# Attention and token/channel mixer on one core: batch 1's channel product by seven half-size products, and a new order at the close of that stage

## The chip, the cores and the metric

The kernel runs on one core of a Trainium2 chip. Of the core's engines, TensorE (PE) multiplies matrices into PSUM, VectorE (DVE) and ScalarE (ACT) read PSUM and write SBUF, GpSimd (POOL) issues the loads of the inputs here, and SyncE (SP) issues the transposing transfers and the stores. The metric is the device time of one launch in microseconds (us). Before the change the median of three runs was 354.32 us (354.26 to 354.45).

## The reference, cut to what matters

There are 8 batches of 12 heads, 448 tokens and 64 features per head; the model width is 768, the token layer is 256 wide and the channel layer 1536.

```python
scores = q @ k.T / sqrt(64) - log(448)
x = sigmoid(scores) @ v                        # per head, then heads side by side: 448 x 768
h = relu(x.T @ w_tok1) @ w_tok2                # mixes tokens, 448 -> 256 -> 448
u = x + h.T
out = u + relu(u @ w_ch1) @ w_ch2              # mixes channels, 768 -> 1536 -> 768
```

The kernel takes its inputs as float32, computes in float16 with float32 accumulation, and writes float32.

## The kernel before, in words

**Cycles.** A cycle is one third of a batch (four heads), so there are 24, numbered c, with batch b = c // 3 and third u = c % 3. The tiles are placed by hand, and every engine carries out its instructions in the order in which the code issues them; nothing is reordered by a planner. Cycle c computes the scores of (b, u) in seven groups (`qk`, L178: four matmuls into a PSUM tile of two banks, then a sigmoid on ACT), the product with v of the cycle before (`av`, L200, PSUM tiles xa, copied to xT by DVE), the token layer of two cycles before (`tok_tail` and `tok1`, tiles tk, ReLU on ACT), and its way back (`ytrans`, L302, tiles yt, which DVE adds to xT to give ut).

**Channel layer.** When the three thirds of a batch are in ut, its first channel product gives h2 = relu(u w_ch1), and its second product gives the output. The second product is spread over the next batch's cycles, one output pair per cycle (`ch2_pair`, L575), and the last 64 tokens go to `ch2_last` (L610).

**Two forms of the first product.** Batches 0 and 1 do it directly: `ch1` (L334) takes one of 12 blocks of 128 channels and makes six matmuls of 448 columns for it (batch 0 partly with 64 x 64 quarters). The later batches use `ch1_seven` (L432), a scheme of the Strassen kind: both matrices are cut in halves, the weights' sums s1, s2, s4 and one difference are made once (`weight_sums`, L398), the tokens' sums once per batch (`token_sums`, L418), and seven products of half the size replace eight. Each product n has three parts a, b, c of 256 channels, so 18 matmuls of 224 columns. Parts a and b share a two-bank tile of the scores' PSUM ring; c and the single parts take one of four other banks. The products 1, 6, 7, 4 are accumulated one on the other in one tile and 5, 3 in a second one, so each waits until the value before it has been copied out: 1, 6 and 5 by ACT into tiles pt, 7 and 3 by DVE with an addition and a ReLU, 4 by a ReLU on ACT. `ORDER` (L931) says in which order the parts run.

**PSUM.** The eight banks are two score tiles of two banks, and four single banks m0 to m3. `bank` (L84) hands these out: first by the written list `OPENING_BANKS`, then in rotation from `at_bank`, which the code sets at places. A new tile in a bank waits until the last reader of the tile before it is done.

**Cycles 6 to 8** (L935 to L987) run between the opening and the steady loop. `work` deals out the pieces of `pending` between the scores: in cycles 6 and 7 the rest of batch 0's second product (20 pieces), in cycle 8 the whole of batch 1's first product (24 half blocks). With each piece one entry of `copies` is carried out (the relayouts of k and q of batch 3 on DVE and their transposes on SP, `through_dma`, L143), or else one of `early`, the nine weight sums. The other three, `late`, change part of c1 in place, which batch 1's direct product still reads, and run in cycle 9.

**Steady loop** (L989 on). In each third cycle of a batch the output pair and the last tokens come first, then the sevens; `ytrans` stands between the sevens' 3c and 4c. The next cycle opens with two score groups and the first turn of an output pair in banks 2 and 3. `gated_loads` (L857) lets POOL start the loads for later batches after it has copied two columns of the freshly transposed q.

Of the kernel before, what the change touches and what calls it, by code (L numbers as in the profile page):

```python
# [13 lines left out]
SUB = mybir.AluOpType.subtract  # L14
# [9 lines left out]
NU = 3  # L24
NS = 224
BY_GROUP = [0, 1, 6, 7, 2, 3, 8, 9, 4, 5, 10, 11]
OPENING_BANKS = "20130130130130213021302130213021313021213021302130202130123102302132132032"


@with_exitstack  # L30
def kernel(
# [13 lines left out]
    B, H, S, E = q.shape  # L45
# [4 lines left out]
    NCB = CC // 128  # L50
# [17 lines left out]
    c1 = pc.tile([128, NDB, CC], FP16, name="c1")  # L68
# [13 lines left out]
    at_bank = [0]  # L82
# [95 lines left out]
    def qk(b, u, j):  # L178
        att[b, u, j] = pa.tile([128, 2, S], FP16, tag="att", bufs=10, name=f"att_{b}_{u}_{j}")
        ps = pp.tile([128, 2, 512], FP32, tag="qk", bufs=2, name=f"qk_{b}_{u}_{j}")  # L180
        for g in range(2):
            for hi in range(2):
                nc.tensor.matmul(  # L183
                    out=ps[64 * g : 64 * g + 64, hi, 0:S],
                    lhsT=tr[b, "k"][64 * hi : 64 * hi + 64, u, j, 64 * g : 64 * g + 64],
                    rhs=tr[b, "q"][64 * hi : 64 * hi + 64, u, :, 64 * g : 64 * g + 64],
                    start=True,
                    stop=True,
                )
        nc.scalar.activation(  # L190
            out=att[b, u, j][:, :, :],
            in_=ps[:, :, 0:S],
            func=SIGMOID,
            bias=bias_t[:, :],
            scale=att_scale,
        )
# [3 lines left out]
    def av(b, u, j0=0, j1=NJ):  # L200
        if j0 == 0:
            xa[b, u] = [
                bank([128, 512], FP32, f"xa_{b}_{u}_{g}")
                for g in range(2)
            ]
        ps = xa[b, u]
        for j in range(j0, j1):
            for g in range(2):
                for hi in range(2):
                    nc.tensor.matmul(  # L210
                        out=ps[g][64 * hi : 64 * hi + 64, 0:S],
                        lhsT=raw[b, "v"][64 * g : 64 * g + 64, u, hi, j, :],
                        rhs=att[b, u, j][64 * g : 64 * g + 64, hi, :],
                        start=(j == 0),
                        stop=(j == NJ - 1),
                    )
        if j1 == NJ:
            for g in range(2):
                nc.vector.tensor_copy(  # L219
                    out=xTs[b % 2][:, u, g, 0:S], in_=ps[g][:, 0:S]  # L220
                )
            if NU * b + u >= N_FIRST:
                nc.vector.tensor_copy(
                    out=xTs[b % 2][:, u, :, S:512], in_=xTs[b % 2][:, u, :, S - 64 : S]
                )
# [172 lines left out]
    def weight_sums():  # L398

        low, high = slice(0, NU), slice(NU, NDB)  # L400
        first, second = slice(0, MC), slice(MC, CC)
        s1, s2, s4 = sums

        def one(out, in0, in1, op):
            return [
                lambda d=d: nc.vector.tensor_tensor(
                    out=out[:, d, :], in0=in0[:, d, :], in1=in1[:, d, :], op=op
                )
                for d in range(NU)
            ]  # L410

        return [
            *one(s1, c1[:, high, second], c1[:, low, second], ADD),
            *one(s2, s1, c1[:, low, first], SUB),
            *one(s4, c1[:, high, first], s2, SUB),
        ], one(c1[:, low, second], c1[:, low, first], c1[:, low, second], SUB)

    def token_sums(b, u0=0, u1=NU):  # L418

# [316 lines left out]
    def pieces_ch1(b, cb0=0):  # L736
        for cb in range(cb0, NCB):
            for d in range(0, NDB, 3):
                yield 3 * S, lambda cb=cb, d=d: ch1(b, cb, d, d + 3)

    def pieces_ch2(b, groups):
        for t, half in groups:
            for n in range(0, NCB, 3):
                yield 3 * DH, lambda t=t, half=half, n=n: ch2(b, t, half, n, n + 3)

    def pieces_last(b):
        for n in range(0, NCB, 3):
            yield 3 * DH, lambda n=n: ch2_last(b, n, n + 3)
# [121 lines left out]
    ONE_RUN = 3 * NU  # L870
# [3 lines left out]
    for c, cb in ((N_FIRST, 3), (N_FIRST + 1, 8)):  # L874
# [3 lines left out]
        copies = []  # L878
# [49 lines left out]
            load(2, "v", v, 1, NU)  # L928
            gated_loads(b)

    ORDER = "1ab 2a 2b 1c 6ab 5ab 2c 6c 5c 7ab 3ab 7c 4ab 3c"  # L931
    SEVENS = [(int(x[0]), x[1:]) for x in ORDER.split()]
    pending, copies = [], []
    early, late = weight_sums()
    for c in range(2 * NU, ONE_RUN):  # L935
        b, u = divmod(c, NU)
        before, ahead = divmod(c - 1, NU), divmod(c - 2, NU)


        if c in (2 * NU, 2 * NU + 2):  # L940
            first = c
            if c == 2 * NU:
                pending, shares = [*pieces_ch2(0, by_half[2:]), *pieces_last(0)], [15, 15]
            else:
                pending, shares = list(pieces_ch1(1)), [30]
            total = sum(w for w, f in pending)
            spent = 0

        def work(share):
            goal = 3 * sum(shares[: c - first]) + share * shares[c - first]  # L950
            done = 0
            while pending and spent + done < total * goal / 90:
                w, f = pending.pop(0)
                f()
                done += w
                if copies:
                    copies.pop(0)()
                elif early:
                    early.pop(0)()
            return done  # L960

        qk(b, u, 0)
        qk(b, u, 1)
        av(*before)
        xtrans_dma(*before)
        qk(b, u, 2)
        if c == 2 * NU + 2:
            copies += through_dma(3, 0)[NU + 1 :]
        spent += work(1)
        qk(b, u, 3)  # L970
        qk(b, u, 4)
        tok_tail(*ahead)
        tok1(*ahead, with_scores=True)
        if c == 2 * NU + 1:
            copies = through_dma(3, 0)[: NU + 1]
        spent += work(2)
        if c == 2 * NU + 2:
            utrans(b - 1)
        qk(b, u, 5)
        qk(b, u, 6)  # L980
        spent += work(3)
        if c + 1 == ONE_RUN:
            at_bank[0] = 0
        ytrans(*ahead)
        if u == 2:
            gated_loads(b)
    assert not copies and not pending and not early  # L987

    for c in range(ONE_RUN, N_CYCLES):  # L989
        b, u = divmod(c, NU)  # L990
        before, ahead = divmod(c - 1, NU), divmod(c - 2, NU)

        X, Y = 2, 0
        at_bank[0] = X
        turn0, turn1, rest = ch2_pair(b - 2, u)
        part = len(turn1) * 2 // 3
        qk(b, u, 0)
        qk(b, u, 1)  # L1000
        for f in turn0:
            f()
        qk(b, u, 2)
        if copies:
            copies.pop(0)()
            copies.pop(0)()
        if u == 2:
            utrans(b - 1)
        at_bank[0] = Y
        av(*before, 0, 4)  # L1010
        qk(b, u, 3)
        av(*before, 4, NJ)
        xtrans_dma(*before)
        if u == 2:
            token_sums(b - 1)
        qk(b, u, 4)
        for f in turn1[:part]:
            f()
        qk(b, u, 5)
        for f in turn1[part:]:  # L1020
            f()
        at_bank[0] = Y
        tok_tail(*ahead)
        qk(b, u, 6)
        tok1(*ahead, with_scores=True)
        rest()
        while late:
            late.pop(0)()
        if u == 1 and copies:
            copies.pop(0)()  # L1030
            copies.pop(0)()
        if u == 0 and LATER < b + 1 < B or u == 1 and b + 1 == LATER:
            copies = through_dma(b + 1, 0)
        if u == 2:
            at_bank[0] = Y + 1
            for w, f in pieces_last(b - 2):
                f()
            step = ch1_seven(b - 1, (1, 3, 0, 2, 0))
            for at, (n, gs) in enumerate(SEVENS):
                step(n, gs)  # L1040
                if copies and at in (1, 3):
                    copies.pop(0)()
            ytrans(*ahead, (2, 0))
            step(4, "c")
        else:
            at_bank[0] = Y
            ytrans(*ahead)
        if u == 2 and b + 1 < B:
            gated_loads(b)
    assert not copies  # L1050
# [25 lines left out]
    token_sums(B - 1, 2, NU)  # L1076
    at = at_bank[0]
    m = [(at + n) % 4 for n in range(4)]
    step = ch1_seven(B - 1, (m[2], m[3], m[0], m[1], m[0]))
    for n, gs in SEVENS:  # L1080
        step(n, gs)
    at_bank[0] = m[1]
    ch2(B - 1, 0, 0, 0, 6)
    step(4, "c")
    at_bank[0] = m[2]
    ch2(B - 1, 0, 0, 6, NCB)
    for t, half in groups[1:]:
        for n in range(0, NCB, 3):
            ch2(B - 1, t, half, n, n + 3)
# [32 lines left out]
```

## Time and profile before

| | us |
|---|---|
| median of three runs | 354.32 |
| profiled execution, its own time | 354.0 |
| its span on the core | 352.2 |
| cycles 6 to 8, first score to the first of cycle 9 | 63.30 to 102.55 |
| one steady cycle, c = 16 | 191.39 to 199.69 |
| the seven products in cycle 11, without yt | 129.32 to 140.87 and 141.62 to 142.20 |
| last batch's tail, first seven to the end of PE's work | 321.31 to 348 |

A row of the timeline gives the start of a group of instructions, how long it lasted, the engine, the line of the code, the operation with the tiles that it writes and reads, and the count; in brackets stands how long the engine was idle before it, and what it waited for. A matmul's recorded duration is its passage through the array; how far apart matmuls are shows in the distance of starts. The granted clock of TensorE was 1.00 in all the stretches between 64 and 108 us.

### The profile page before, as it was taken

What the parts mean: (1) busy time and instruction counts of PE and PEld (TensorE: products, weight loads), DVE (VectorE), ACT (ScalarE), POOL (GpSimd) and SP (SyncE); (2) the same over time, 40 slices, a digit from 0 to 9 for tenths busy, and PEclk for the clock granted to TensorE, in tenths of its full rate; (3) what the DMA queues carried; (4) which work ended last, traced back from release to release, by engine and by line L of the source; (5) the groups of instructions that cost most, each with busy time, mean ns of one, the idle gap of its engine ahead of it and who ended that gap; (6) DMA issues with size and microseconds to landing.
All of it is one profiled execution on the core that took longest, in us unless ns stands there. A gap on an engine that the chain in (4) does not pass through costs nothing.

```text
span 352.2 us, 10131 instructions
## 1 busy us (share of the span) xinstructions
PE 342.4 (97%) x4423; PEld 237.2 (67%) x4423; DVE 199.7 (57%) x395; ACT 205.1 (58%) x263; POOL 56.9 (16%) x98
## 2 busy tenths in 40 slices
PE   7999999999999999999999999999999999999995
PEld 4655565555556679656886679766886679557953
DVE  3476558656546566458575566558563366518621
ACT  4996844566258854888348854888348853111400
POOL 8893430220040000400040000300010000000000
PEclk9999999999999999999999999999999999999999
DMA  7999999999999597998979597999984390055214
GB/s 118 171 179 200 206 204 199 166 208 251 169 173 193 90 171 162 159 170 154 201 113 195 133 183 160 164 163 158 206 106 94 85 157 24 5 117 110 50 45 112
DMA packets 104379, 52.16 MB, mean 148 GB/s; under 512 B 76432, under 2 KB 101264, under 8 KB 104336
## 3 DMA queue, kind: packets, MB, share of 16 engines
q1 hardware_dynamic: 78944, 29.70, 47.3%
q0 software_dynamic: 25168, 21.50, 40.1%
q8 instruction: 34, 0.56, 0.6%
q10 hardware_dynamic: 224, 0.33, 0.3%
q14 instruction: 9, 0.07, 0.1%
HBM read 43.45 MB, written 11.01 MB: 155 GB/s over the span
## 4 chain that ended last, share of the span: by engine, by line
PE 77%; DMA 7%; DVE 6%; POOL 4%; ACT 2%; issue 2%; DVEq 0%; ACTq 0%; POOLq 0%
PE c L364 11%; PE c L537 10%; PE c_ab L487 9%; PE qk L183 7%; PE xa L210 7%; PE c L341 7%; PE c L598 5%; PE c L622 5%; PE c_c L487 5%; PE tk L286 5%; DVE h L517 4%; PE yt L309 3%; DMA c<-in_moe_w_ch_dram 3%; DMA xn<-xT 2%; DMA w<-in_moe_w_tok_dram 2%
## 5 line engine op out<-in xcount | busy, mean ns | idle before, releaser
L190 ACT ACTIVATE att<-qk,att_bias 128x896 f16<-128x896 f32 x168 | 155.7, 1015 | 46.9 <-PE qk L183 46.4
L183 PE MATMUL qk<-tr_q,tr_k 64*64 64x448 f16 x672 | 58.9, 356 | 0.5 <-ACT att L190 0.2
L219 DVE CAST xT<-xa 128x448 f16<-128x448 f32 x48 | 27.7, 618 | 40.1 <-PE xa L210 40.1
L364 PE MATMUL c<-c,h 64*64 64x384 f16 x960 | 47.1, 323 | 1.1 <-DVE ut L316 1.0
L560 DVE TENSOR_TENSOR o<-un,c 128x384 f32<-128x384 f16 x42 | 23.3, 554 | 41.8 <-PE c L598 20.7
L487 PEld LDWEIGHTS <-c 128*128 128x128 f16 x432 | 41.0, 98 | 2.9 <-issue 1.8
L210 PE MATMUL xa<-att,raw_v 64*64 64x448 f16 x672 | 40.3, 349 | 0.2 <-DVE ut L316 0.2
L537 PE MATMUL c<-c,h 128*128 128x384 f16 x216 | 37.9, 326 | 0.6 <-DVE ut L316 0.5
L364 PEld LDWEIGHTS <-h 64*64 64x64 f16 x960 | 30.0, 107 | 12.3 <-issue 2.1
L183 PEld LDWEIGHTS <-tr_k 64*64 64x64 f16 x672 | 21.3, 105 | 18.8 <-issue 12.1
L508 ACT ACTIVATE pt_ab<-c_ab 128x896 f32<-128x896 f32 x18 | 16.5, 917 | 29.0 <-PE c_ab L487 29.0
L487 PEld LDWEIGHTS <-sum 128*128 128x128 f16 x324 | 31.1, 98 | 0.0
L537 PEld LDWEIGHTS <-h 128*128 128x128 f16 x216 | 20.3, 98 | 15.2 <-issue 2.1
L316 DVE TENSOR_TENSOR ut<-xT,yt 128x448 f16<-128x448 f16 x48 | 27.4, 613 | 2.4 <-PE yt L309 2.4
L210 PEld LDWEIGHTS <-raw_v 64*64 64x64 f16 x672 | 21.8, 107 | 10.3 <-issue 1.1
L859 POOL COPY gate<-tr_q 128x2 f16<-128x2 f16 x6 | 1.4, 239 | 168.9 <-DMA tr_q<-rel_q 168.9
L341 PE MATMUL c<-ut,c 128*128 128x448 f16 x120 | 24.6, 353 | 0.4 <-DMA c<-in_moe_w_ch_dram 0.4
L300 ACT ACTIVATE h<-tk 128x256 f16<-128x256 f32 x42 | 14.2, 408 | 16.6 <-PE tk L286 16.6
L598 PE MATMUL c<-c,h 128*128 128x384 f16 x120 | 22.0, 326 | 0.0
L309 PE MATMUL yt<-w,h 128*128 128x448 f16 x96 | 21.9, 353 | 0.0
L286 PE MATMUL tk<-xn,w 128*128 128x256 f16 (+1 forms) x156 | 21.8, 274 | 0.1
L352 DVE TENSOR_SCALAR h<-c 128x448 f16<-128x448 f32 x24 | 14.5, 621 | 10.9 <-PE c L341 10.1
(86 smaller groups left out, 402.5 us busy)
## 6 DMA issues: line engine op xcount, KB each, us to landing
out_dram<-o SPq DMA_DIRECT2D x48, 192.0 KB, 3.1
c<-in_moe_w_ch_dram POOLq DMA_DIRECT2D x4, 1152.0 KB, 15.8
raw_k<-in_k_dram POOLq DMA_DIRECT2D x10, 336.0 KB, 7.7
raw_q<-in_q_dram POOLq DMA_DIRECT2D x10, 336.0 KB, 11.2
raw_v<-in_v_dram POOLq DMA_DIRECT2D x10, 336.0 KB, 5.7
out_dram<-o SPq DMA_DIRECT2D x15, 96.0 KB, 2.4
raw_q<-in_q_dram POOLq DMA_DIRECT2D x12, 112.0 KB, 5.0
raw_k<-in_k_dram POOLq DMA_DIRECT2D x12, 112.0 KB, 5.1
```

The source lines that it names most:

```text
L183: nc.tensor.matmul(out=ps[64 * g : 64 * g + 64, hi, 0:S], lhsT=tr[b, "k"][64 * hi : 64 * hi + 64, u, j, 64 * g : 64 * g + 64], rhs=tr[b, " ...
L190: nc.scalar.activation(out=att[b, u, j][:, :, :], in_=ps[:, :, 0:S], func=SIGMOID, bias=bias_t[:, :], scale=att_scale,)
L210: nc.tensor.matmul(out=ps[g][64 * hi : 64 * hi + 64, 0:S], lhsT=raw[b, "v"][64 * g : 64 * g + 64, u, hi, j, :], rhs=att[b, u, j][64 * g : ...
L219: nc.vector.tensor_copy(out=xTs[b % 2][:, u, g, 0:S], in_=ps[g][:, 0:S])
L286: nc.tensor.matmul(out=ps[tcb], lhsT=w1[rows, t, cols], rhs=xn[b, u][rows, :, t, :], start=(t == 0 and not with_scores), stop=(t == (2 if ...
L309: nc.tensor.matmul(out=ps[:, 0:S], lhsT=h1[b, u][:, tcb, g, :], rhs=w2[:, tcb, :, :], start=(tcb == 0), stop=(tcb == 1),)
L316: nc.vector.tensor_tensor(out=uts[b % 2][:, db, 0:S], in0=xTs[b % 2][:, u, g, 0:S], in1=ps[:, 0:S], op=ADD)
L341: nc.tensor.matmul(out=ps[:, 0:S], lhsT=c1[:, BY_UNIT[d], 128 * cb : 128 * cb + 128], rhs=uts[b % 2][:, BY_UNIT[d], 0:S], start=(d == 0), ...
L364: nc.tensor.matmul(out=ps[p][m : m + 64, 0:n], lhsT=lhsT(p, part, m), rhs=rhs(p, part), start=(first and turn == 0), stop=(last and turn = ...
L487: nc.tensor.matmul(out=ps[:, g, p, :], lhsT=weights[n][:, d, 128 * cb : 128 * cb + 128], rhs=moving[n][:, d, :], start=(n in (1, 5, 2) and ...
L537: nc.tensor.matmul(out=ps[:, 0:DH], lhsT=h2[b][:, BY_GROUP[cb], 128 * t : 128 * t + 128], rhs=c2[:, BY_GROUP[cb], cols], start=(cb == 0), ...
L598: nc.tensor.matmul(out=ps[p][:, 0:DH], lhsT=h2[b][:, BY_GROUP[n], 128 * t : 128 * t + 128], rhs=c2[:, BY_GROUP[n], DH * p : DH * p + DH], ...
```

## The change

Batch 1's first channel product goes through `ch1_seven` as well, at the end of cycle 8. For that all twelve weight sums are made in cycles 6 to 8, one for each piece of work that has no relayout to carry out, and the token sums of batch 1 are made in cycle 8. Batch 0's twenty output pieces are dealt over the three cycles 6, 7 and 8 instead of two. The banks of these cycles are no longer taken from the written list: xa, tk and yt start at bank 0 each time, and the output groups alternate between banks 3 and 2.

In all stages of sevens 7c is moved ahead of 3ab, and 4c is the last of the sevens, ahead of `ytrans`. The single parts' banks change from (1, 3, 0, 2, 0) to (2, 3, 0, 1, 0) (c's two chains, then 2a, 2b, 2c), and yt takes banks 0 and 1 instead of 2 and 0. The output pair of the next cycle keeps banks 2 and 3; the tiles that it follows there are now c's two chains. In the tail 4c stands ahead of the first output group instead of in its middle.

```diff
-OPENING_BANKS = "20130130130130213021302130213021313021213021302130202130123102302132132032"
+OPENING_BANKS = "201301301301302130213021302130213130212130213021302021301"
...
             *one(s4, c1[:, high, first], s2, SUB),
-        ], one(c1[:, low, second], c1[:, low, first], c1[:, low, second], SUB)
+            *one(c1[:, low, second], c1[:, low, first], c1[:, low, second], SUB),
+        ]
...
-    ORDER = "1ab 2a 2b 1c 6ab 5ab 2c 6c 5c 7ab 3ab 7c 4ab 3c"
+    ORDER = "1ab 2a 2b 1c 6ab 5ab 2c 6c 5c 7ab 7c 3ab 4ab 3c 4c"
...
+    def sevens(b, banks=(2, 3, 0, 1, 0)):
+        step = ch1_seven(b, banks)
+        for at, (n, gs) in enumerate(SEVENS):
+            step(n, gs)
+            if copies and at in (1, 3):
+                copies.pop(0)()
...
-    early, late = weight_sums()
+    early = weight_sums()
+    lane = [0]
...
-        if c in (2 * NU, 2 * NU + 2):
+        if c == 2 * NU:
             first = c
-            if c == 2 * NU:
-                pending, shares = [*pieces_ch2(0, by_half[2:]), *pieces_last(0)], [15, 15]
-            else:
-                pending, shares = list(pieces_ch1(1)), [30]
+            pending, shares = [*pieces_ch2(0, by_half[2:]), *pieces_last(0)], [10, 10, 10]
...
                 w, f = pending.pop(0)
+                if len(pending) % 4 == 3:
+                    lane[0] ^= 1
+                at_bank[0] = 2 + lane[0]
                 f()
...
+        at_bank[0] = 0
         av(*before)
...
+        at_bank[0] = 0
         tok_tail(*ahead)
...
             utrans(b - 1)
+            token_sums(b - 1)
         qk(b, u, 5)
         qk(b, u, 6)
         spent += work(3)
-        if c + 1 == ONE_RUN:
-            at_bank[0] = 0
+        if u == 2:
+            sevens(b - 1)
+        at_bank[0] = 0
         ytrans(*ahead)
...
         rest()
-        while late:
-            late.pop(0)()
...
-            step = ch1_seven(b - 1, (1, 3, 0, 2, 0))
-            for at, (n, gs) in enumerate(SEVENS):
-                step(n, gs)
-                if copies and at in (1, 3):
-                    copies.pop(0)()
-            ytrans(*ahead, (2, 0))
-            step(4, "c")
-        else:
-            at_bank[0] = Y
-            ytrans(*ahead)
+            sevens(b - 1)
+        at_bank[0] = Y
+        ytrans(*ahead)
...
-    step = ch1_seven(B - 1, (m[2], m[3], m[0], m[1], m[0]))
-    for n, gs in SEVENS:
-        step(n, gs)
+    sevens(B - 1, (m[2], m[3], m[0], m[1], m[0]))
     at_bank[0] = m[1]
-    ch2(B - 1, 0, 0, 0, 6)
-    step(4, "c")
-    at_bank[0] = m[2]
-    ch2(B - 1, 0, 0, 6, NCB)
+    for n in range(0, NCB, 3):
+        ch2(B - 1, 0, 0, n, n + 3)
```

## The prediction

> **What bounds the kernel now.** I read the page's engine shares first, then TensorE's timeline around the change, then what DVE and the transfers do at the places where TensorE waits. PE below is TensorE.
>
> ```profile
> PE 342.4 (97%) x4423; PEld 237.2 (67%) x4423; DVE 199.7 (57%) x395; ACT 205.1 (58%) x263; POOL 56.9 (16%) x98
> PE 77%; DMA 7%; DVE 6%; POOL 4%; ACT 2%; issue 2%; DVEq 0%; ACTq 0%; POOLq 0%
> ```
>
> PE is the bound, so a column of matmul taken off it counts, and so does each PE gap. PE's timeline (start, us, line, output<-inputs, count): batch 1's first channel product in cycle 8, and the same product of batch 2 in sevenths, closed by yt and product 4c:
>
> ```profile
> 86.09 4.71 PE L341 MATMUL c<-ut,c 128*128 128x448 f16 x24
> 92.01 4.70 PE L341 MATMUL c<-ut,c 128*128 128x448 f16 x24
> 97.15 4.71 PE L341 MATMUL c<-ut,c 128*128 128x448 f16 x24
> ...
> 129.32 1.32 PE L487 MATMUL c_ab<-ut,c 128*128 128x224 f16 x12
> ...
> 141.62 0.74 PE L487 MATMUL c_c<-diffs,c 128*128 128x224 f16 x6
> 142.29 0.57 PE L183 MATMUL qk<-tr_q,tr_k 64*64 64x448 f16 x8
> 143.36 1.49 PE L364 MATMUL c<-c,h 64*64 64x384 f16 x32 [0.49 <-DVE ut L316]
> ```
>
> The last line is a gap: the next cycle's output pair waits for bank 2, which yt took and DVE empties late. It recurs:
>
> ```profile
> 183.47 1.50 PE L364 MATMUL c<-c,h 64*64 64x384 f16 x32 [0.29 <-DVE ut L316]
> 223.07 1.50 PE L364 MATMUL c<-c,h 64*64 64x384 f16 x32 [0.25 <-DVE ut L316]
> 301.80 2.11 PE L537 MATMUL c<-c,h 128*128 128x384 f16 x12 [0.52 <-DVE ut L316]
> ```
>
> DVE's timeline: a relayout that waits for its load in cycle 7, yt's evacuation, and the three late weight sums in cycle 9 ahead of an evacuation. Then PE, waiting for that evacuation:
>
> ```profile
> 73.15 1.14 DVE L316 TENSOR_TENSOR ut<-xT,yt 128x448 f16<-128x448 f16 x2
> ...
> 78.84 0.62 DVE L125 COPY rel_k<-raw_k 128x896 f16<-128x896 f16 x1 [1.48 <-DMA raw_k<-in_k_dram]
> ...
> 110.67 1.49 DVE L406 TENSOR_TENSOR c<-c 128x768 f16<-128x768 f16 x3
> 112.08 1.14 DVE L316 TENSOR_TENSOR ut<-xT,yt 128x448 f16<-128x448 f16 x2
> ```
>
> ```profile
> 113.27 0.94 PE xa L210 x14
> ```
>
> (From the chain.) It shows what happens when xa and yt share banks 0 and 1 and DVE is late: xa waits.
>
> **The change part by part**, against the profiled execution: span 352.2, its own time 354.0, 0.3 below the median of 354.32. I take the difference off the median.
>
> *The product itself (cycle 8).* Removed: 12 blocks of 6 matmuls of 448 columns. Ten of them elsewhere (start 36.20, 2.07 long, the last one 0.363) are 0.1894 apart: 72 x 0.1894 = 13.64 us. Added: 7 x 18 = 126 matmuls of 224 columns; twelve take 1.15 (129.32 to the next start, 130.48), so 0.0958 each, 12.07 us. PE: -1.57. The evacuations change from 12 DVE ones of 0.62 to eight by ACT (four of 0.92, four of 0.54) and fourteen by DVE (0.28 to 1.09); they lie beside PE as in cycle 11, whose same block runs without a gap over 0.05.
>
> *Work before it.* Batch 0's twenty output pieces, ten in each of cycles 6 and 7, become 7, 7 and 6 in cycles 6 to 8: no PE time, but cycles 6 and 7 shrink from 10.1 and 10.5 to about 8.4 and 8.7. ACT's seven scores at 0.90 spacing and two ReLUs of 0.33 need 7.0, so it stays below PE.
>
> *Banks 0 and 1 in cycles 6 to 8: a wait added.* xa, tk and yt are now all put there, and xa opens a cycle only two score groups (0.40) behind yt; later cycles have a 1.30 us turn of the output pair between. yt starts, 0.63 later DVE adds its first half, the second ends at about 1.77 (72.52 to 74.29), while xa would start at 1.25 (73.77). By hand:
> - Cycle 6: bank 1 holds the last opening output group, copied by DVE from 63.40 to 63.96; xa wanted 63.70: +0.3.
> - Cycle 7: yt about 71.15, second half added by 72.95, xa wanted at 72.4: +0.6.
> - Cycle 8: the relayout of k stands on DVE ahead of the copies of the output group and yt. Its load is issued at 70.43 behind a gate off PE's path and lands at 78.84, so that does not move with PE. Behind it, by row spacing: two relayouts 0.53 each, output copy 0.48, relayout 0.53, one weight sum 0.47, ut 0.53, ut 0.61 to its end: 82.52. xa wanted 81.6: +1.0. If the load lands earlier, since the first output stores (72.33 before) come about 3 us later, this shrinks; I take 0.25 less.
>
> From xa at 82.57 to the next cycle: 18.10 in the trace (84.45 to 102.55), less 13.82 for the removed matmuls with their changes of shape, plus 12.1, 3.43 for six pieces with their ends, and 0.3 for changes of shape: 20.1, so cycle 9 starts at 102.7, or 102.45 with the earlier load, against 102.55. Sum of these three items: -0.1, with ends -0.8 (no wait in cycle 8) and +1.0. The gain on PE is mostly spent on this wait.
>
> *Other queues in cycles 6 to 8.* The q relayouts reach DVE at about 85.4; their load lands at 72.4 + 11.2 = 83.6. SP issues the transposed q at about 87.5 instead of 89.97, landing 6.1 later, 8 us before use. POOL's gate waits for that landing, so its loads come no later. DVE then has the q copies, the four token sums (1.94), the last sums and the final copies (1.14), ending at about 91.5; the first seven's addition is due at 91.95. No wait; two us more on DVE would show as a delay of 2c, which needs bank 0.
>
> *The three late sums (cycle 9).* They leave 1.49 of DVE work ahead of ut. Cycle 10 lasts 8.85 (110.85 to 119.70), cycles 9, 16, 19 and 22 last 8.30: -0.55. They are paid for in cycles 7 and 8 above.
>
> *Closing the stage.* 4c moves ahead of yt, and yt to banks 0 and 1, emptied long before. The pair's banks 2 and 3 are now last read by 4c's ReLU and 3c's addition. From the start of 7ab: 7ab ends 1.15, 7c 1.73, 3ab 2.88, 4ab 4.03, 3c 4.60, 4c 5.18, yt 5.93, two score groups 6.33. DVE: 7ab from 1.42, 7c from 2.85, 3ab from 3.68, 3c 5.11 to 5.72. ACT: 4ab 4.23 to 5.15, 4c 5.38 to 5.92. So 4ab (waits 7ab's addition, 2.51), 4c (7c's, 3.49), scores (5.15 and 4.77) and pair (5.92) find their banks free; the tightest margin is 0.35 to 0.4. What is late next is ut, ending at 7.1, with xa due at 7.9. The cycles after a stage lasted 8.99 (142.29 to 151.28), 8.79, 8.75 and 8.51, and the tail's pair started 0.68 after 4c's end: 0.69 + 0.49 + 0.45 + 0.21 + 0.68 = 2.52. Of the first I credit 0.3: cycle 13 already waits for xn (issued 148.03, landing 8.7 later) behind the loads, so an earlier arrival waits longer there. -2.1, ends -2.5 and 0.
>
> *Last batch.* 4c moves ahead of its output groups. Before, the third matmul waited for 4ab's ReLU (332.45 + 0.92 = 333.37, due 333.15): now 4c covers it. -0.25.
>
> Sum: -0.1 - 0.55 - 2.1 - 0.25 = -3.0.
>
> A rule to weigh. POOL's gate copy at 69.89 took 0.50 beside a weight sum, 0.19 to 0.31 elsewhere; four sums now run from 69.85 on, and I leave its time as it is. The Trainium skill's SBUF — State Buffer, Who interferes with whom, says that a DVE instruction with two SBUF inputs holds off a GpSimd instruction that reads SBUF until it ends. By that rule the gate could wait for one more sum, and the sum would be about -2.5; the longer gate copy agrees with it.
>
> **The rivals.**
> - *The load is not in the way* (lands before DVE gets to it, about 77.1): cycle 8 loses nothing, xn keeps pace: -0.8 - 0.55 - 2.5 - 0.25 = -4.1, 350.2. For it: fewer stores beside it. Against: 1.48 us of waiting in the row.
> - *The closing wait only changes its name* (4c's ReLU in place of ut): -0.1 - 0.55 - 0 - 0.25 = -0.9, 353.4. For it: margins of only 0.4. Against: four closes all waited for DVE, not ACT.
> - *Slower: the DVE queue of cycles 7 and 8.* Each us that k lands later than 78.84 delays ut, xa and everything behind by a us, since the relayouts stand ahead of them. It decides from a landing at 81.8 on. If k landed only with q (83.6), 4.8 - 3.0 = +1.8: 356.1. For it: the trace's k and q loads spread over 5.9 to 11.2 us. Against: the queue's order.
> - *A wash*: cycles 6 to 8 end at their upper bound (+1.0) and the closes give only 0.7, because the scores after a close run into ACT: +1.0 - 0.55 - 0.7 - 0.25 = -0.5, 353.8. For it: ACT is busy for 7.0 of 8.3. Against: cycles 16, 19 and 22 hold 8.30 with the same scores.
>
> **How the numbers follow.** Forecast 0.55; first rival 0.13; second 0.17; slower one 0.10; the wash 0.05. Likeliest: 354.32 - 3.0 = 351.3, its own range 350.3 to 352.6. The overall range leaves out the slower rival and some of the first: 350.0 to 353.7. A measurement tells 0.2% (0.7 us) from no change: faster 0.83 (forecast, first and nearly all of the second), same 0.07, slower 0.10.
>
> **What would show it.** Cycle 8: 126 matmuls 0.096 apart, no c<-ut,c of 448 columns after 58. PE xa waiting for DVE ut at the starts of cycles 7 and 8, the latter near 82.5, with the k relayout at 78 to 79. Cycle 9 starting within 1 us of 102.5. Cycle 10 at 8.3. No wait of L364 for ut after stages, cycles there at 8.3 to 8.5. The prediction is wrong if xa in cycle 8 waits much longer or not at all, if pairs wait for ACT's ReLU, or if scores in cycles 6 to 8 wait for ACT.

## The result, and the profile after

The changed kernel takes 351.29 us (median of six, 350.07 to 352.89) against 354.38 for the kernel before in the same comparison (353.79 to 355.17): a ratio of 0.9911, with an interval of 0.9884 to 0.9938. The profiled execution took 350.74, its span is 349.0, against 354.0 and 352.2 before. Single executions of the changed kernel lie up to 2.8 apart, so what one cause is worth is read below from the lengths of the cycles in the profiles, and the medians are only asked whether they agree. Cycle 6 starts at 62.8 to 64.3 in the profiles of this document, and differs also where the code before it is the same (63.30 in the kernel before, 63.77 in the one with the close alone). Where whole profiles are compared, the time is therefore counted from cycle 6 to the end of the span: 288.9 before and 285.6 after.

The page of the changed kernel, engine shares (PEld is TensorE's loading of weights, beside its matmuls) and the chain by engine:

```profile
PE 340.3 (98%) x4477; PEld 239.4 (69%) x4477; DVE 201.4 (58%) x401; ACT 211.1 (60%) x271; POOL 57.3 (16%) x98
PE 81%; DMA 10%; POOL 4%; ACT 2%; DVE 2%; issue 1%; ACTq 0%; POOLq 0%
```

PE is still the bound. DVE's share of the chain went from 6 to 2%, that of the transfers rose from 7 to 10%. PE's timeline, cycle 7 to the start of cycle 9:

```profile
73.09 1.51 PE L210 MATMUL xa<-att,raw_v 64*64 64x448 f16 x26 [0.16 <-DVE ut L316]
...
82.24 1.51 PE L210 MATMUL xa<-att,raw_v 64*64 64x448 f16 x26 [0.15 <-DVE ut L316]
...
89.36 1.32 PE L488 MATMUL c_ab<-ut,c 128*128 128x224 f16 x12
...
100.87 0.74 PE L488 MATMUL c_c<-diffs,c 128*128 128x224 f16 x6
101.44 0.92 PE L309 MATMUL yt<-w,h 128*128 128x448 f16 x4
102.30 0.57 PE L183 MATMUL qk<-tr_q,tr_k 64*64 64x448 f16 x8
102.70 1.47 PE L364 MATMUL c<-c,h 64*64 64x384 f16 x32
```

The two xa lines are the added wait: the first two xa matmuls start at 72.56 and 81.71, and the third 0.53 later instead of with them. What this costs shows below, where yt is moved and the wait goes: 0.55 in each of cycles 7 and 8, and 0.33 in cycle 6, where bank 1 is emptied late. The last line is the cure of the close: the pair starts 0.40 after the scores, without a wait. No L364 line waits for ut any more; what is left from cycle 9 on are two waits of tk for xn:

```profile
155.27 0.30 PE L267 MATMUL tk<-xn,w 64*64 64x256 f16 x4 [0.26 <-DMA xn<-xT]
234.09 0.30 PE L267 MATMUL tk<-xn,w 64*64 64x256 f16 x4 [0.33 <-DMA xn<-xT]
```

DVE's timeline: the relayout of k waits for its load less long than before, and ut of cycle 9 (110.42) follows the output additions directly.

```profile
78.04 1.15 DVE L125 COPY rel_k<-raw_k 128x896 f16<-128x896 f16 x2 [0.79 <-DMA raw_k<-in_k_dram]
...
81.04 1.15 DVE L316 TENSOR_TENSOR ut<-xT,yt 128x448 f16<-128x448 f16 x2 [0.40 <-PE yt L309]
...
110.42 1.15 DVE L316 TENSOR_TENSOR ut<-xT,yt 128x448 f16<-128x448 f16 x2
```

The lengths of the cycles, from first score to first score on PE's timelines of the two:

| | before | after | difference |
|---|---|---|---|
| cycles 6 to 8 | 39.25 | 38.92 | -0.33 |
| 10 | 8.85 | 8.30 | -0.55 |
| 12, 15, 18, 21 | 8.99, 8.79, 8.75, 8.51 | 8.30 each | -1.84 |
| 13 (waits for xn in both) | 8.77 | 8.76 | -0.01 |
| 19 | 8.30 | 8.82 | +0.52 |
| 23, to the tail's pair | 23.15 | 22.50 | -0.65 |
| from there to PE's last matmul group | 45.81 | 45.37 | -0.44 |

With 0.1 for the rest they make the 3.2 by which the span is shorter.

### The profile page after: what moved, and what is told of

Its sections match the earlier page's. It is cut to its first block, busy times and chain, and to the rows that moved or that the text cites. A ratio compares the mean times of both kernels' runs of the same rounds, so it can differ in the third digit from the quotient of the medians.

```text
span 349.0 us, 10254 instructions
## 1 busy us (share of the span) xinstructions
PE 340.3 (98%) x4477; PEld 239.4 (69%) x4477; DVE 201.4 (58%) x401; ACT 211.1 (60%) x271; POOL 57.3 (16%) x98
## 4 chain that ended last, share of the span: by engine, by line
PE 81%; DMA 10%; POOL 4%; ACT 2%; DVE 2%; issue 1%; ACTq 0%; POOLq 0%
PE c_ab L488 14%; PE c L364 10%; PE c L538 10%; PE c_c L488 8%; PE qk L183 7%; PE xa L210 7%; DMA xn<-xT 5%; PE c L599 5%; PE c L623 5%; PE tk L286 4%; PE yt L309 4%; DMA c<-in_moe_w_ch_dram 3%; PE c L341 3%; DMA w2s<-in_moe_w_tok_dram 2%; ACT att L190 2%; POOL raw_k L114 1%
## 5 line engine op out<-in xcount | busy, mean ns | idle before, releaser
L183 PE MATMUL qk<-tr_q,tr_k 64*64 64x448 f16 x672 | 58.1, 356 | 0.5 <-ACT att L190 0.2
L488 PEld LDWEIGHTS <-c 128*128 128x128 f16 x504 | 47.8, 98 | 1.9 <-issue 1.8
L364 PE MATMUL c<-c,h 64*64 64x384 f16 x960 | 46.6, 322 | 0.0
L509 ACT ACTIVATE pt_ab<-c_ab 128x896 f32<-128x896 f32 x21 | 19.3, 917 | 30.5 <-PE c_ab L488 30.5
L488 PEld LDWEIGHTS <-sum 128*128 128x128 f16 x378 | 36.3, 98 | 0.0
L364 PEld LDWEIGHTS <-h 64*64 64x64 f16 x960 | 28.1, 107 | 11.9
L210 PEld LDWEIGHTS <-raw_v 64*64 64x64 f16 x672 | 20.9, 107 | 11.6 <-issue 1.6
L511 ACT ACTIVATE h<-c_ab 128x896 f16<-128x896 f32 x7 | 6.4, 917 | 24.4 <-PE c_ab L488 24.4
L518 DVE TENSOR_TENSOR h<-pt_ab,c_ab 128x896 f16<-128x896 f32 x14 | 15.1, 1081 | 9.6 <-PE c_ab L488 9.6
```

The source lines that it names most:

```text
L183: nc.tensor.matmul(out=ps[64 * g : 64 * g + 64, hi, 0:S], lhsT=tr[b, "k"][64 * hi : 64 * hi + 64, u, j, 64 * g : 64 * g + 64], rhs=tr[b, " ...
L210: nc.tensor.matmul(out=ps[g][64 * hi : 64 * hi + 64, 0:S], lhsT=raw[b, "v"][64 * g : 64 * g + 64, u, hi, j, :], rhs=att[b, u, j][64 * g : ...
L364: nc.tensor.matmul(out=ps[p][m : m + 64, 0:n], lhsT=lhsT(p, part, m), rhs=rhs(p, part), start=(first and turn == 0), stop=(last and turn = ...
L488: nc.tensor.matmul(out=ps[:, g, p, :], lhsT=weights[n][:, d, 128 * cb : 128 * cb + 128], rhs=moving[n][:, d, :], start=(n in (1, 5, 2) and ...
```

## The experiments

**The close alone, and the product alone.** Two kernels split the change into its halves.

*Close alone:* the kernel before with

```diff
-    ORDER = "1ab 2a 2b 1c 6ab 5ab 2c 6c 5c 7ab 3ab 7c 4ab 3c"
+    ORDER = "1ab 2a 2b 1c 6ab 5ab 2c 6c 5c 7ab 7c 3ab 4ab 3c 4c"
...
-            step = ch1_seven(b - 1, (1, 3, 0, 2, 0))
+            step = ch1_seven(b - 1, (2, 3, 0, 1, 0))
...
-            ytrans(*ahead, (2, 0))
-            step(4, "c")
...
+        at_bank[0] = Y
+        ytrans(*ahead)
...
```

(The tail's lines, left out here, are those of the change.)

> The kernel before with the new close of the stage alone (7c ahead of 3ab, 4c ahead of yt, banks 2, 3, 0, 1, 0 for the single parts and 0, 1 for yt, the tail likewise); batch 1's product stays direct and the three late sums stay in cycle 9. Theory (the closing wait is DVE's ut in bank 2 and goes with the new banks and order): cycles 12, 15, 18 and 21 fall from 8.99, 8.79, 8.75 and 8.51 to 8.30, the tail's pair starts 0.65 earlier, the last batch saves 0.25 to 0.46; cycle 10 stays at 8.85. In all -2.5 to -3.0. Rival (batch 1's product is what pays, the close is worth little): -0.5 or less, with waits for ACT's ReLU in place of ut.

Measured: 351.87, ratio 0.9925 (0.9901 to 0.9948). Cycles 12, 15, 18 and 21 are 8.31, 8.30, 8.30 and 8.30, cycle 10 stays at 8.85, cycle 19 takes 8.80, cycles 6 to 8 39.26. Its span is 350.0, 2.2 less than before, but cycle 6 started 0.5 later in this execution; from there on it takes 286.2, 2.7 less, as the medians have it, and within the 2.5 to 3.0 expected. The close gives most of the gain, and gives it without batch 1's new product. Cycle 19 takes back 0.5, which was not expected; cycle 13 gave 0.28.

*Old close:* the changed kernel with the old order, banks and tail.

```diff
...
-    def sevens(b, banks=(2, 3, 0, 1, 0)):
+    def sevens(b, banks=(1, 3, 0, 2, 0)):
...
-            sevens(b - 1)
+            step = sevens(b - 1)
+            ytrans(*ahead, (2, 0))
+            step(4, "c")
...
```

> The changed kernel with the old close everywhere (7c behind 3ab, yt between 3c and 4c, old banks, the old tail), batch 1 by sevens as changed. Theory: the waits for ut come back, now also in cycle 9: cycles 9, 12, 15, 18, 21 at 8.5 to 9.0, the tail 0.65 and 0.25 to 0.46 later; +2.5 to +3.5 on the changed kernel, about 354. Rival (the close is worth little): within 0.5 of the changed kernel.

Measured: 353.52, ratio 0.9988 (0.9961 to 1.0015), no longer to be told from the kernel before. Cycles 9, 12, 15, 18 and 21 take 8.53, 8.78, 8.79, 8.53 and 8.52, the tail's pair waits for ut (0.53). From cycle 6 on it takes 288.1, 2.5 more than the changed kernel; by the medians of the two comparisons it is 2.0, less than the 2.5 to 3.5 expected. The rival, a close worth little, is out on both sides.

**Order or banks.** Each of the next two takes back one half of the close.

*4c behind yt, new banks:*

```diff
-    ORDER = "1ab 2a 2b 1c 6ab 5ab 2c 6c 5c 7ab 7c 3ab 4ab 3c 4c"
+    ORDER = "1ab 2a 2b 1c 6ab 5ab 2c 6c 5c 7ab 7c 3ab 4ab 3c"
...
+            ytrans(*ahead, (0, 1))
+            step(4, "c")
...
```

> The changed kernel with its new banks, but 4c behind yt as before (the tail unchanged). Theory: 4c ends 0.75 later, its ReLU on ACT ends 6.7 after the start of 7ab, the pair wants bank 2 at 6.33, so 0.35 to 0.4 of waiting for ACT in the cycles 9, 12, 15, 18 and 21 (8.65 to 8.7 each) and 0.8 in the tail: +2 to +2.7 in all, and a wait of the output pair for ACT h instead of DVE ut. Rival (the banks alone are the cure): 8.30 in these cycles, no difference.

Measured: 353.12, ratio 0.995 (0.9929 to 0.9972). Cycles 9, 12, 15, 18 and 21 take 8.62 each, 0.32 more than 8.30, a little under the 0.35 to 0.4 expected. ACT's timeline gives 4c's ReLU in cycle 8's stage, PE's the pair that follows, and the tail's pair names its releaser:

```profile
101.81 0.54 ACT L511 ACTIVATE h<-c_c 128x448 f16<-128x448 f32 x1 [0.99 <-PE c_c L488]
```

```profile
102.40 1.49 PE L364 MATMUL c<-c,h 64*64 64x384 f16 x32
...
299.90 2.11 PE L538 MATMUL c<-c,h 128*128 128x384 f16 x12 [0.63 <-ACT h L511]
```

The ReLU ends at 102.35 and the pair starts at 102.40, 0.70 after the scores instead of 0.40. The span is only 0.9 above that of the changed kernel, not 2 to 2.7: its opening reached cycle 6 0.6 earlier in this execution, and cycles 13 and 19 are 0.34 and 0.52 shorter, as tk asks for xn later behind the longer cycles 12 and 18. From cycle 6 on it takes 287.1, 1.5 more than the changed kernel.

*Old banks, new order:*

```diff
-    def sevens(b, banks=(2, 3, 0, 1, 0)):
+    def sevens(b, banks=(1, 3, 0, 2, 0)):
...
-        ytrans(*ahead)
+        ytrans(*ahead, (2, 0) if u == 2 else ())
```

> The changed kernel with its new order (7c ahead of 3ab, 4c ahead of yt) but the old banks 1, 3, 0, 2, 0 for the single parts and 2, 0 for yt (the tail unchanged). Theory: the pair finds bank 2 held by yt's first half, which DVE adds from 5.97 to 6.55 after the start of 7ab, while the pair wants it at 6.33: 0.25 of waiting for DVE ut in each of the cycles 9, 12, 15, 18, 21 and 0.65 in the tail, +1.5 to +2.2 in all. Rival (the order alone is the cure): 8.30 in these cycles, no difference.

Measured: 353.21, ratio 0.996 (0.9939 to 0.998). Cycles 9, 12, 15, 18 and 21 take 8.68, 8.52, 8.53, 8.65 and 8.52, and the waits are for DVE's ut (0.19 and 0.16 in cycles 9 and 18, 0.53 in the tail; in the other three the pair starts 0.60 after the scores instead of 0.40). So neither half is enough: with the banks alone the pair waits for ACT, with the order alone for DVE.

**The product itself.** The changed kernel with batch 1's product made directly at the same place.

```diff
-            sevens(b - 1)
+            for cb in range(NCB):
+                at_bank[0] = 2 + cb % 2
+                ch1(b - 1, cb)
```

> The changed kernel, but at the end of cycle 8 batch 1's product is made directly, by 72 matmuls of 448 columns in banks 2 and 3, and everything else is as changed. Part of the weights has been replaced by their difference by then, so batch 1's output is computed from other weights; the amount of work is that of the direct product. Theory: cycle 9 starts 1.5 to 1.7 later (13.64 against 12.07 on TensorE). Rival (DVE and ACT set the pace of the block, not TensorE): less than 0.8.

Measured: 352.12, ratio 0.9938 (0.9909 to 0.9967). Two rows of PE's timeline hold it:

```profile
90.93 14.06 PE L341 MATMUL c<-ut,c 128*128 128x448 f16 x72
104.83 0.92 PE L309 MATMUL yt<-w,h 128*128 128x448 f16 x4
```

From 90.93 to 104.83 are 13.90, against 12.08 for the sevens (89.36 to 101.44): 1.82 more, 0.25 above the prediction. The direct matmuls are 0.189 apart here too; what is added are two waits, 0.165 and 0.095, ahead of the second and the third block's first matmul (92.24 and 93.48). The second block's bank is held by the last output copy, which DVE ends at 92.18, and the third waits for the first block's ReLU (92.80 to 93.43), which stands on DVE behind that copy and a weight sum. So the rival has a small share. Without the two waits the block takes 13.64 and the product is worth 1.56, as predicted. Cycle 9 starts 2.84 later after cycle 8's start than in the changed kernel; the other 1.0 is a longer wait of xa, as k landed at 80.10 in this execution. The 1.5 to 1.7 expected for the start of cycle 9 did not allow for either.

**The late sums.** The kernel before with the three sums of cycle 9 behind yt.

```diff
         rest()
-        while late:
-            late.pop(0)()
...
             ytrans(*ahead)
+        while late:
+            late.pop(0)()
```

> The kernel before with the three late weight sums of cycle 9 moved behind yt, so that DVE adds ut first. Theory (the sums delay ut, and xa of cycle 10 waits for it): cycle 10 falls from 8.85 to 8.30 to 8.40, -0.5. Rival (something else in cycle 10): it stays at 8.85.

Measured: 353.59, ratio 0.998 (0.9965 to 0.9996); cycle 10 takes 8.30. The sums delayed ut, and ut delayed xa; the 0.55 is theirs, and it could be had without the rest of the change. (Its span is 352.2 as before, but its cycle 6 starts 0.9 later.)

**The load of k.** The changed kernel with the order of batch 3's two loads exchanged.

```diff
-        for t, src in (("k", k), ("q", q)):
+        for t, src in (("q", q), ("k", k)) if b == 1 else (("k", k), ("q", q)):
```

> The changed kernel with the loads of batch 3's q and k exchanged, so that k lands when q did, at about 81.4 instead of 78.04. Theory (the slower rival's mechanism: the relayouts of k stand on DVE ahead of ut, and xa waits for ut): xa of cycle 8 waits until about 85.2 and cycle 9 starts 2.5 to 3.0 later. Rival (the load is covered by other work): cycle 9 within 0.5 of the changed kernel.

Measured: 357.32 (353.17 to 360.49), ratio 1.0052 (1.0017 to 1.0087): slower than before the change. The profiled execution is the longest of the ten, 360.49, so what it shows is larger than in the median. DVE, then PE:

```profile
85.46 1.15 DVE L125 COPY rel_k<-raw_k 128x896 f16<-128x896 f16 x2 [7.79 <-issue]
...
87.98 1.14 DVE L316 TENSOR_TENSOR ut<-xT,yt 128x448 f16<-128x448 f16 x2
```

```profile
81.84 0.57 PE L183 MATMUL qk<-tr_q,tr_k 64*64 64x448 f16 x8
88.65 3.35 PE L210 MATMUL xa<-att,raw_v 64*64 64x448 f16 x28 [6.24 <-DVE ut L316]
```

k landed at 73.3 + 12.1 = 85.4, not 81.4, so DVE stood for 7.79 (the view calls it issue, but the landing is what ends it), ut followed 2.5 later, and xa waited 6.4 from 82.24. That is the mechanism, with the late transfer mis-sized. In this execution it costs more than the wait: the windows (stretch and its length in us, busy time of PE, PEld, DVE, ACT and POOL, TensorE's granted clock, share and rate of the transfers) show the clock at half until 94.7, some 6 us after the matmuls begin again.

```profile
84.00:88.00 4.00, 0.00 (x0) 0.00 (x0) 2.54 (x6) 0.24 (x1) 0.00 (x0) 0.56 0.27 92
88.00:90.00 2.00, 1.35 (x14) 0.66 (x17) 1.13 (x3) 0.00 (x0) 0.00 (x0) 0.50 0.85 205
...
94.00:96.00 2.00, 2.00 (x23) 1.06 (x21) 1.23 (x3) 0.83 (x1) 0.00 (x0) 0.82 0.70 131
```

The 28 xa matmuls with the next scores' start take 2.77 (88.65 to 91.42) instead of 1.32. Cycle 8 lasts 30.0 against 20.99. The difference of 9.0 is the 6.4 of waiting, less the 0.55 that the changed kernel loses there too, and about 3 of slow clock. No profile shows the nine other executions; their mean granted clock lies at 0.989 to 0.998, highest in the shortest (353.17), and at 0.984 in this one. The Trainium skill's TensorE: Matmul & The Clock Gate, Part 1, says that an idle window of about 3.4 us halves PE's clock and a busy one of that length restores it; the 0.50 after 6.2 idle agrees with it, and in a kernel below a wait of 3.06 was enough.

**yt early.** The added wait was then attacked: the changed kernel with yt ahead of the third share of work in cycles 6 and 7.

```diff
+        if u < 2:
+            at_bank[0] = 0
+            ytrans(*ahead)
         spent += work(3)
         if u == 2:
             sevens(b - 1)
-        at_bank[0] = 0
-        ytrans(*ahead)
+            at_bank[0] = 0
+            ytrans(*ahead)
```

> The changed kernel with yt ahead of the third share of work in cycles 6 and 7, so that 1.0 us of output matmuls stands between yt and the xa that takes its banks. Theory (xa waits for DVE's addition of yt's second half, 0.44 each in cycles 7 and 8): both waits go, cycle 9 starts 0.7 to 0.9 earlier relative to cycle 6. Rival 1 (the load of k and its relayouts hold DVE anyway): the wait in cycle 8 stays, 0.4 gained at most. Rival 2 (yt now comes before ACT's ReLU of tk): yt waits instead, nothing gained.

Measured: 350.88, ratio 0.9888 (0.9847 to 0.9928). Cycles 7 and 8 take 8.61 and 20.44 instead of 9.16 and 20.99, and no xa of cycles 7 and 8 waits; cycles 6 to 8 take 37.82, 1.1 less, more than the 0.7 to 0.9 expected, since each wait of 0.44 by the rows cost 0.55. The span is 348.9, no shorter than the changed kernel's: cycle 16 takes 9.28 with a wait of 0.79 for xn, and cycle 6 started 0.4 later in this execution.

**yt early, and the relayouts behind it.** Here the eight steps of batch 3's k and q (six relayouts and two transposing transfers) start only in the last share of cycle 7, and the last opening group lies in bank 3.

```diff
-        if c == 2 * NU + 2:
-            copies += through_dma(3, 0)[NU + 1 :]
...
-        if c == 2 * NU + 1:
-            copies = through_dma(3, 0)[: NU + 1]
         spent += work(2)
...
+        if c == 2 * NU + 1:
+            copies = through_dma(3, 0)
         spent += work(3)
```

> The changed kernel with yt ahead of the third share of work in cycles 6 and 7, the relayouts of batch 3's k and q started only behind it in cycle 7, and the last opening output group in bank 3 instead of 1. Theory: none of the three waits of xa for DVE is left and a late k no longer stands ahead of ut; cycles 6 to 8 take 37.6 to 37.9 instead of 38.9, whenever k lands before 82; about 350.2 against 351.3. Rival (k's relayouts only hold the next thing on DVE, xT, and tk waits for it): cycle 8 as long as with yt early alone, 20.4, or longer.

Measured: 354.98, ratio 1.0016 (1.0 to 1.0032): the whole gain is gone. The profiled execution is the shortest of the twelve, 352.82, and shows only a part of the loss: from cycle 6 on it takes 287.8, 2.2 more than the changed kernel. SP's timeline (SPq: SP issues a transfer), then POOL's, then PE's:

```profile
90.92 4.36 SPq L323 DMA_TRANSPOSE un<-ut  x1
95.38 1.18 SPq L655 DMA_DIRECT2D out_dram<-o  x2
96.61 3.39 SPq L138 DMA_TRANSPOSE tr_q<-rel_q  x1
```

```profile
101.89 0.19 POOL L860 COPY gate<-tr_q 128x2 f16<-128x2 f16 x1 [27.57 <-DMA tr_q<-rel_q]
```

```profile
118.00 0.30 PE L267 MATMUL tk<-xn,w 64*64 64x256 f16 x4 [2.55 <-DMA xn<-xT]
```

The transpose of q now comes behind that of u and two stores on SP, 8.2 later than in the changed kernel (88.44). POOL's gate opens at 101.89 instead of 95.58, the loads collide with cycle 9's xn, which takes 10.8 from issue to landing instead of 5.7, and cycle 10 lasts 11.04. Cycle 8 also lost 0.82 to xn, so cycles 6 to 8 take 38.66, although no xa waits any more. Neither theory nor rival had this: it is the queue past which the step was moved. What the eleven longer executions lose beside this is not shown.

*The same with later loads of q:*

```diff
-            if b + 2 < B:
+            if b + 2 < B and (b == 1 or t == "k"):
...
+        if u == 0 and b + 1 < B:
+            nc.gpsimd.tensor_copy(out=gate[:, :], in_=xn[before][:, 0, 0, 0:2])
+            load(b + 1, "q", q, 0, NU)
```

> As the kernel with yt and the relayouts moved, and in addition the load of a later batch's q is issued only when the next cycle's xn has landed, from batch 4's q on. Theory (xn waits behind three loads in the transfers' queues, and tk waits for xn in cycles 13, 16 or 19): xn lands 3 to 5 after its issue instead of 7.7 to 8.8, and cycles 13, 16 and 19 take 8.30 each: 0.9 to 1.4 less than without. Rival (the delay of xn is not the loads' doing, or q now comes late): cycles 13 and 19 stay at 8.5 to 8.8, or a later cycle waits for the relayouts of q.

Measured: 355.09, ratio 1.0031 (1.0012 to 1.0051). Cycles 13, 16 and 19 do take 8.30 each, as the theory has it, but the second half of the rival holds as well: batch 4's q is loaded from 116.21 on, DVE waits 5.09 for it in cycle 11, xT stands behind that relayout, and tk waits 3.06 for xT. PE's rows:

```profile
127.22 0.30 PE L267 MATMUL tk<-xn,w 64*64 64x256 f16 x2 [3.06 <-DVE xT L219]
...
128.48 1.46 PE L286 MATMUL tk<-xn,w 128*128 128x256 f16 x6
```

Cycle 11 lasts 27.83 instead of 22.55, and the waits, 3.3 with the next one of 0.23, are not all of it: the granted clock is 0.50 from 127.54 to 130.95, which costs about 1.7 (the six matmuls of the second row take 1.46 where cycle 6 has 0.83). So a slow clock after a wait shows in an execution of median length as well (355.06). The wait of 2.55 in the kernel before this one left the clock at 1.00. Cycle 10 lasts 8.89 instead of 11.04, with xn of cycle 9 landing after 7.4 instead of 10.8: without q's load beside it most of that collision is gone.

**yt early, relayouts left in place.** Yt early and the opening group in bank 3 only.

```diff
-OPENING_BANKS = "201301301301302130213021302130213130212130213021302021301"
+OPENING_BANKS = "201301301301302130213021302130213130212130213021302021303"
```

> The changed kernel with yt ahead of the third share of work in cycles 6 and 7 and the last opening output group in bank 3 instead of 1; the relayouts stay where the change has them. Theory: the waits of xa for DVE in cycles 6 to 8 go (cycle 6 loses 0.16, cycles 7 and 8 0.44 each) and SP and POOL keep their order, so cycles 6 to 8 take 37.6 to 37.9 and cycle 10 stays at 8.30: 350.2 to 350.9. Rival (the loss seen when the relayouts were moved is due to yt's new place): cycle 10 waits for xn again and the time is 353 or more.

Measured: 350.47, ratio 0.9899 (0.9872 to 0.9926). Cycles 6 to 8 take 38.01 and cycle 10 8.49, so the loss above was the relayouts'. Cycle 6 is shorter by 0.33, cycle 7 by 0.55, cycle 8 by 0.03 only (20.96; 20.44 in the run with yt early alone). The traces show why: here k landed 2.37 ahead of cycle 8's first score, at 78.55, there 3.14 ahead. Behind k's relayouts DVE adds ut from 80.63 to 81.77, and the third xa matmul, due at 81.33, starts at 81.83; with yt early alone ut ended at 81.21, ahead of xa at 81.53. So the theory failed in cycle 8: with yt's own latency out of the way, the load of k sets the wait. Cycles 13, 16 and 19 take 8.73, 8.79 and 8.84, with waits for xn.

**q's transpose sooner.** The last one, with the loads moved out of xn's way from the other side.

```diff
-        if copies:
-            copies.pop(0)()
+        for _ in range(min(len(copies), 4 if u == 2 else 2)):
             copies.pop(0)()
```

> As the kernel with yt early and the last opening group in bank 3, and in the third cycle of every batch all four remaining steps of the next batch's q (relayouts and the transposing transfer) run behind the first scores, ahead of the transpose of u, instead of two there and two between the sevens. Theory (POOL's loads start when the transposed q lands, and xn of the next cycle queues behind them): the loads start about 8 earlier, xn of cycles 12, 15 and 18 lands 3 to 5 after its issue, cycles 13, 16 and 19 take 8.30: 0.5 to 1.4 less than without. Rival: SP's queue now delays the transposes of u and of the same cycle's xn, and cycles 12, 15 and 18 wait for xn instead: no gain, or a loss of up to 2.

Measured: 349.6 (348.88 to 350.74), ratio 0.9876 (0.9856 to 0.9897), span 348.1: the fastest of all by its median and its span, though its interval overlaps those of the kernels with yt early. SP's lines of cycle 11, and the xn of cycle 12, show the new order:

```profile
123.94 3.96 SPq L138 DMA_TRANSPOSE tr_q<-rel_q  x1
127.95 3.71 SPq L323 DMA_TRANSPOSE un<-ut  x1
131.77 1.31 SPq L233 DMA_TRANSPOSE xn<-xT  x1
...
146.65 1.23 SPq L233 DMA_TRANSPOSE xn<-xT  x1
```

The gate of cycle 11 opens at 129.93 instead of 139.06. Cycles 13, 16 and 19 take 8.30, 8.30 and 8.31. The rival's cost is there, but covered: xn of cycle 11 takes 14.1 to land, at 145.9, and is wanted at about 147; xn of cycle 12 still takes 7.6, not the 3 to 5 expected, but lands at 154.26, 0.7 before tk needs it; the last load of q landed at 153.50. So the gain in cycle 13 hangs on 0.7.

## Why the prediction was right, point by point

It said 351.3 and -3.0; measured were 351.29 and -3.1 by the medians, -3.2 by the spans. Where the time goes was right in kind. That the sum agrees to 0.1 is luck: its terms are off by up to 0.2 in both directions, and single executions lie 2.8 apart.

- *The product:* -1.57 predicted, and -1.56 measured from the matmuls themselves; with the direct one in the same place the block is 1.82 longer, 0.26 of it two waits for DVE. The kernel before had no such waits, but its three pieces, from the first matmul to whatever follows, take 4.64 + 4.63 + 4.55 = 13.82, so 1.74 went there; the prediction uses this 13.82 for the start of cycle 9 and 13.64 for the product.
- *The added wait:* +0.3, +0.6 and +0.75 predicted for cycles 6, 7 and 8; measured by taking the waits away, 0.33 (bank 3 for the last opening group), 0.55 and 0.55 (yt early). Right in place and kind, in sum 0.2 too long; the prediction's remark that the gain on PE is mostly spent on this wait held. In cycle 8 the predicted reason was the chain behind k; in the profiled execution DVE had 0.40 of slack there, so the wait was yt's own latency, as in cycle 7. That k becomes the reason when it lands later is shown by the exchange of the loads, by the direct product, where it landed at 80.10, and by yt early with the opening group in bank 3.
- *Cycles 6 to 8 together:* -0.1 predicted, -0.33 measured (-1.74 and the three waits, 1.43, make -0.31), within the bounds of -0.8 and +1.0. So the product that the change is named after gives little here; most comes from the close.
- *The late sums:* -0.55 predicted and measured, and shown by moving them alone.
- *The close:* -2.1 predicted. The waits went entirely, -2.49, and 0.52 came back in cycle 19 as a wait for xn, a net of -1.97. The place was wrong: 0.39 was expected back in cycle 13, where xn came earlier by as much as the cycle did. That xn is what is late next was right; that the loss has a similar size in another cycle is luck.
- *The last batch:* -0.25 predicted, -0.44 measured for all behind the tail's pair; of the 0.2 more, which part is the undivided first output group was not tested.
- *The rule on DVE and POOL:* from the gate's start to the first load 0.54 passed both before (69.89 to 70.43) and after (70.60 to 71.14), so its 0.5 did not come; the gate copy took 0.37.
- *The rivals:* the closing wait that only changes its name is what the kernel with 4c behind yt does, at 0.32 a cycle; the change escapes it by the order. The slower one is real as a mechanism: with k behind q the changed kernel takes 357.3, against the rival's 356.1, and the slow clock after the wait was not in it. It did not happen because k is issued first and landed 0.8 earlier than before. The first rival, in which cycle 8 loses nothing, came near its condition (DVE waited only 0.79 for k and then had slack), but yt's own latency was left. The wash is out: the closes gave 1.97 net and not 0.7.

## What to carry to other kernels

A wait at the close of a stage can have two owners in a row: look up who last reads each bank that the next stage wants, and when, for the order and for the banks; here either alone left 0.2 to 0.4 a cycle. Where a step with a transfer is moved, walk down the queue that it is moved past to whatever its landing releases: starting the eight steps of k and q a share later saved the waits of xa that it was meant to save, and the time was that of the kernel before again; its profile shows waits of 3.4 for xn, which came through SP and POOL. A saving that shortens a cycle in front of a transfer shows up as a wait for the transfer, so follow the landing times before adding up savings.

## What was not expected of the hardware

A wait of TensorE can cost half as much again as it lasts. After 6.2 us without matmuls it ran at 0.50 of its clock for about 6 us, in the longest execution of its kernel; after a wait of 3.06 it did so for 3.4 us, in an ordinary one; after 2.55 the clock stayed at 1.00. And the landing of one and the same transfer moves: with k issued first, k of batch 3 was there at 77.8 to 80.7 in thirteen profiles, and xn took between 3.0 and 14.1 from issue to landing, the most of it with the loads issued ahead of it.
